# Seven products for eight in the second half of a recurrent-attention and dense-layer kernel

## Chip, cores and metric

One core of one Trainium2 chip. The metric is the device time of one execution in microseconds (us); the time before is the median of three runs.

## What is computed

The reference has two parts. First a recurrent attention over four batches, eight heads, 768 steps and a head size of 48, with a 48x48 state for each head; then a two-layer network on its 3072 rows of 384 numbers, whose nonlinearity is h - tanh(h).

```
for t in range(S):                       # S = 768, B = 4, H = 8, D = 48
    cur = einsum('bhd,bhe->bhde', u * k[t], v[t])
    y[t] = einsum('bhd,bhde->bhe', r[t], state + cur)
    state = w * state + einsum('bhd,bhe->bhde', k[t], v[t])
x = y transposed and reshaped to (3072, 384)
h = x @ w_in                             # 384 -> 2048
g = h - tanh(h)
out = g @ w_out                          # 2048 -> 384
```

All is float32 (the two weight matrices arrive as 64-bit floats and are converted on the chip).

## The kernel before

**Attention.** The 768 steps are cut into 12 chunks of 64 (`SHORT`). A *unit* is one chunk of two batches, so there are 24 units (`unit(n)`, n from 0 to 23; the chunk is n // 2). A unit's steps are: TensorE transposes of r and k into PSUM (`turn`, L644); scaling of r on VectorE into `rT` (L648) and a copy of k on ScalarE into `kT` (L657); 64-wide products of the state with r into `y_ps` and of k with r into `lev` (both in `levels`, issued by `put`, L602); the select of `lev` into `at` on VectorE (L781); the products of `at` with v and of k with v (`outputs`, `to_state`, L602); and the copies out on ScalarE (`to_xt`, `to_rest`, through `given`, L729 and L731), from which GpSimd's DMA queue moves a remainder into place (L745). The state is added and decayed on VectorE (L751, L790).

The two PSUM tiles of attention have two banks each: `x_ps` takes the transposes and then `lev`; `yk_ps` takes `y_ps` and `kv_ps`. Unit 1 has two banks of its own for the first, `x2_ps`, which later serve the output product.

**Dense layer.** Two units are one *block* of 256 rows (`L` = 2), 12 blocks in all. The 2048 columns in the middle are 16 groups of 128 (`NF`), and a *tile* is two groups of one block, so a block has eight tiles. For a tile (`hidden`):

- `h`: 2 x 3 matmuls of 256 columns (L165) into one of two PSUM buffers;
- `act`: five ScalarE passes over 128x512 (L174 to L182);
- `vec`: four VectorE passes over 128x512 (L189 to L195), the last a select into `g` (five buffers);
- `o`: four matmuls of 384 columns (L203), which add into `outs`, two PSUM banks, one for each half of 128 rows of the block.

After the last tile of a group of tiles `empty` moves each bank out: a copy on ScalarE (L222), for the last block a copy on VectorE (L220), or a VectorE sum with what earlier tiles gave (L211). `store` sends the result to memory from GpSimd's queue (L228).

Blocks 0 to 5 (`FIRST` = 6) run while weights still come in: in four passes of four groups each over all six blocks. Blocks 6 to 11 run one after the other, all 16 groups at once (`fs` = (0, 16)). Units 16 to 23 are the attention of blocks 8 to 11 and lie among the tiles of blocks 6 to 9.

**Order.** Every step is a task in `Plan` with an engine, a fixed cost and the tasks that it follows. `order()` simulates the engines with these costs, then tries 1000 random shifts of due times (one fixed seed) and keeps what ends no later; the kernel issues its instructions in the order found. Any change of the tasks therefore changes the order everywhere. While TensorE would idle early on, filler matmuls (`fills`, L539 and L540) keep it running.

A path `anywhere`, for decay factors out of a range, is compiled in but not taken.

Of the kernel before, what the change touches and what calls it, by code (L numbers as in the profile page):

```python
# [11 lines left out]
F32 = mybir.dt.float32  # L12
# [3 lines left out]
AF = mybir.ActivationFunctionType  # L16
ALU = mybir.AluOpType
# [14 lines left out]
C = 128  # L32
# [5 lines left out]
OWN = 1  # L38
SWAP = 2


# [11 lines left out]
class Dims:  # L53
    def __init__(self, r, moe_w_in):
        self.B, self.H, self.S, self.D = r.shape
        self.DM, self.DFF = moe_w_in.shape
        self.NP = self.H // 2
        self.NCH = self.S // C
        self.NU = self.NCH * self.B
        self.NK = self.DM // 128  # L60
        self.NX = self.D // self.NK
        self.NF = self.DFF // 128
        self.NT = L * C
        self.NB = self.NU // L

        self.HEAD = [slice(i * PAD, i * PAD + self.D) for i in range(2)]
# [76 lines left out]
class Dense:  # L143


    def __init__(self, nc, work, gpool, ps_d, shared, out, rows, ps_o=None, last=None):
        self.nc, self.work, self.gpool, self.ps_d, self.ps_o = nc, work, gpool, ps_d, ps_o or (lambda: ps_d)
        self.out, self.rows, self.xts, self.sums, self.last = out, rows, {}, {}, last
        self.d, self.w_in_sb, self.w_out_sb, self.m1b, self.smallb = (
            shared[x] for x in ("dims", "w_in", "w_out", "m1b", "smallb"))  # L150
# [46 lines left out]
    def o(self, t, half):  # L197

        if t.first and half == 0:
            self.outs = [self.ps_o().tile([128, 512], F32, name=f"o{i}", tag=f"o{i}", bufs=1)[:, : self.d.DM]  # L200
                         for i in range(L)]
        for z, i in [(0, half), (1, half)] if t.last else [(half, 0), (half, 1)]:
            self.nc.tensor.matmul(self.outs[i], t.g2[:, z, i * C : (i + 1) * C], self.w_out_sb[:, t.f + z, :],  # L203
                                  start=t.first and z == 0, stop=t.last and z == 1)

    def empty(self, t, i):

        whole, at = t.fs[1] == self.d.NF, (t.j, i)
        if t.fs[0]:
            t.o = self.sums.pop(at) if whole else self.sums[at]  # L210
            self.nc.vector.tensor_tensor(t.o, self.outs[i], t.o, ALU.add)  # L211
            return
        if whole:
            t.o = self.work.tile([128, self.d.DM], F32, name="o", tag="o")
        else:
            t.o = self.sums[at] = self.work.tile([128, self.d.DM], F32, name="part", tag="part", bufs=L * FIRST)
        if t.j == self.d.NB - 1:
            if self.last is not None:
                t.o = self.last[:, i]
            self.nc.vector.tensor_copy(t.o, self.outs[i])  # L220
        else:
            self.nc.scalar.copy(t.o, self.outs[i])  # L222

    def store(self, o, n, z, queue):
# [204 lines left out]
@with_exitstack  # L429
def near(ctx, tc, r, k, v, w, u, out, shared, weights):  # L430

# [11 lines left out]
    ps_a = ctx.enter_context(tc.tile_pool(name="n_ps_a", bufs=1, space=PSUM))  # L443
    ps_d = ctx.enter_context(tc.tile_pool(name="n_ps_d", bufs=2, space=PSUM))

    def fixed(name, shape, dt=F32):
        return const.tile(shape, dt, name=name, tag=name)
# [4 lines left out]
    dense = Dense(nc, work, gpool, ps_d, shared, out,  # L452
                  lambda n: [(n % 2 * 2 + z) * d.S + n // 2 * SHORT for z in range(2)], lambda: later(), shared["last"])
    HALF = [slice(z * SHORT, (z + 1) * SHORT) for z in range(2)]
# [3 lines left out]
    V.memset(rows, 1.0)  # L458
    same = fixed("same", [128, SHORT])
    V.tensor_tensor(same, ident[:, :SHORT], ident[:, SHORT:], ALU.add)  # L460
    by, plus = (work.tile([128, NP, SHORT + 1], F32, name=x, tag=like) for x, like in (("by", "tg"), ("plus", "q")))
# [22 lines left out]
    for z in range(2):  # L484
# [5 lines left out]

    ps, yk_ps = (ps_a.tile([128, 2, 512], F32, name=x, tag=x) for x in ("x_ps", "yk_ps"))

    early = ExitStack()
    x_banks = [ps, early.enter_context(tc.tile_pool(name="n_ps_x", bufs=1, space=PSUM)).tile(
        [128, 2, 512], F32, name="x2_ps", tag="x2_ps")]
    pools = []

    def later():
        if not pools:
            early.close()  # L500
            pools.append(ctx.enter_context(tc.tile_pool(name="n_ps_o", bufs=1, space=PSUM)))
        return pools[0]
    y_ps = yk_ps[:, :, :256].rearrange("e z (p t) -> e z p t", p=NP)
    kv_ps = yk_ps[:, :, 256 : 256 + NP * D].rearrange("d z (p e) -> d z p e", p=NP)
# [96 lines left out]
    def put(*args, **how):  # L601
        T.matmul(*args, skip_group_check=True, **how)  # L602
# [3 lines left out]
    def unit(n):  # L606
# [7 lines left out]
        rt, vt, kw, state = rts[n % (AHEAD + 1)], vts[n % (AHEAD + 1)], kws[n % 2], states[half]  # L614
        r_ps, k_ps = (x_banks[n == 1][:, i] for i in range(2))
        lev, own_lev = (x_banks[n == 1][:, :, at : at + 256].rearrange("s i (p t) -> s i p t", p=NP) for at in (0, 256))
        none = SimpleNamespace(**{x: None for x in "r k v turn rT kw kT rk du own diag state lev cp out xt rest add decay".split()})
# [69 lines left out]

        def levels():
            for p in range(NP if ch else 0):
                for z in range(2):  # L690
                    for i in range(2):
                        put(y_ps[to(i, z), z, p], state[HEAD[i], z, p], t.rT[HEAD[i], p, z],
                            start=p == 0, stop=False)
            for p in range(NP):
                for z in range(2):
                    for i in range(2):
                        put(lev[HALF[z], i, p], t.kT[HEAD[i], p, z], t.rT[HEAD[i], p, z], start=True, stop=True)

# [18 lines left out]
        def to_state():  # L717
            for p in range(NP if more else 0):
                for i in range(2):
                    for z in range(2):  # L720
                        put(kv_ps[i * PAD : (i + 1) * PAD, z, p], kw[HALF[z], 2 * p + i], vt[HALF[z], 2 * p + i, :D],
                            start=True, stop=True)

        def given(out, y):

            if not swap:
                A.copy(out, y)
                return
            A.copy(out[:, 0], y[:, 0])  # L729
            for i in range(2):  # L730
                A.copy(out[i * PAD : (i + 1) * PAD, 1], y[to(i, 1), 1])  # L731

# [24 lines left out]

        free = [b1.cp, b1.diag] if n > 2 else [units[0].cp, units[0].diag] if n == 2 else []
        x.turn = add("PE", .46, lambda: turn(rt, r_ps), [x.r] + free, steps=8)
        x.kw = add("DVE", .47, lambda: V.tensor_tensor(kw[:, :, :D], t.kt[:, :, :D], w_down, ALU.mult), [x.k, downs, b2.out])  # L760
# [12 lines left out]
        else:  # L773
# [4 lines left out]
            x.diag = add("ACT", 1.0, lambda: diagonal(range(H // 2, H)), [now])  # L778
        x.lev = add("PE", (1.35 if swap else 1.75) if ch else .7, levels,
                    [x.kT, x.rT, b2.out] + ([b2.decay, b1.xt, b1.rest, b1.add] if ch else []), steps=128 if ch else 64)  # L780
        x.cp = add("DVE", .64, lambda: V.copy_predicated(t.at, before, lev), [x.lev, b2.out] + ([] if product else [x.diag]))  # L781
# [15 lines left out]

    tiles, stored = [], {}

    def hidden(j, fs, f, due, pace):  # L800
        t = dense.tile(j, fs, f)
        none = SimpleNamespace(g=None, c1=None, c2=None, cp=None, o=None, h=None, s=None, q=None, small=None, th=None, tg=None, empty=[])
        m = len(tiles)
        b1, b2, b5 = (tiles[m - i] if m >= i else none for i in (1, 2, 5))
        x = SimpleNamespace(empty=[])
# [15 lines left out]
        x.cp = add("DVE", .65, lambda: dense.vec(t, "cp"), [x.c2, x.small, x.g])  # L821
        now = add("PE", 1.3, lambda: dense.o(t, 0), [x.cp, converted[piece + 2], b1.o] + b1.empty + ([units[1].cp, units[1].diag] if m == 0 else []), due + 2 * pace, steps=8)
        if m == 0:
# [28 lines left out]
    for n in range(L * (FIRST + 2), d.NU):  # L852
        unit(n)
    for j in range(FIRST, d.NB):
        for f in range(0, d.NF, 2):
            hidden(j, (0, d.NF), f, now, 6.0)
            now += 5.2 + (.95 if j + 2 < d.NB else 0)

# [248 lines left out]
def kernel(  # L1107
# [28 lines left out]
    shared = {"dims": d, "ident": ident, "w_in": w_in_sb, "w_out": w_out_sb, "flag": flag, "last": last, **consts}  # L1136
    with tc.tile_pool(name="stage", bufs=2) as stage:
        weights = Weights(nc, stage, shared, moe_w_in, moe_w_out)
        with tc.manual_schedule():
            near(tc, r, k, v, w, u, out, shared, weights)  # L1140

# [38 lines left out]
```

## Time and profile before

| what | value |
|---|---|
| median of 3 runs | 619.47 us (619.37 to 620.41) |
| profiled execution: span from first to last instruction | 617.3 us |
| what lies around it, by the median of the runs | 2.2 us |
| mean granted TensorE clock | 0.997 |
| TensorE, VectorE, ScalarE, GpSimd busy | 98%, 70%, 65%, 11% |

The profile shows one execution. The page gives its span only; the execution's own device time stands nowhere in it, so the last 2.2 us are the difference to the median. "PE" is TensorE's matmul side, "PEld" its weight loads, DVE is VectorE, ACT ScalarE, POOL GpSimd, SP the sync engine with the main DMA queue. A duration of a matmul is a model from start to end and overlaps the next; how fast a row of them goes is seen in the chain of waits, where each piece is what it adds. For VectorE and ScalarE, too, the mean duration of an instruction is longer than the step to an independent next one: 688 ns for 512 columns, while the chain has 0.60.

### The profile page before, as it was taken

To read this page: it belongs to the slowest core of one execution; us is meant where nothing else is said; L and a number is where in the kernel's file an instruction comes from. 1 tells how busy PE (TensorE), PEld (TensorE's weight loads), DVE (VectorE), ACT (ScalarE), POOL (GpSimd) and SP (SyncE) were. 2 spreads that over 40 slices of the span, in tenths; PEclk is the share of its full clock that TensorE was granted. 3 is DMA by queue.
4 is the path that set the end of the run, shared out by engine and by line. 5 is a ranking of instruction groups with operands and counts; after the bars stand their busy time and mean duration, and the time that the engine had idled before them with its cause. 6 is when DMAs were issued, how large, how long until landed. Compare 5 with 4: busy or idle time off the path is not lost.

```text
span 617.3 us, 13070 instructions
## 1 busy us (share of the span) xinstructions
PE 603.8 (98%) x5215; PEld 444.7 (72%) x5215; DVE 430.4 (70%) x699; ACT 403.6 (65%) x892; POOL 70.5 (11%) x159
## 2 busy tenths in 40 slices
PE   7899999999999999999999999999999999999996
PEld 6667777777777777777777776777777777777774
DVE  5699979999997699766675845657657636445453
ACT  2489789958965667555764855656677666655552
POOL 5001311300000000002132010001101110110100
PEclk9899999999999999999999999999999999999999
DMA  6964495464031000002333112011112100100101
GB/s 126 225 125 92 100 228 109 84 111 133 16 94 52 0 1 2 0 7 46 65 70 67 28 32 53 14 36 37 25 28 48 26 10 1 27 6 1 27 1 30
DMA packets 86318, 33.68 MB, mean 55 GB/s; under 512 B 78536, under 2 KB 80680, under 8 KB 86248
## 3 DMA queue, kind: packets, MB, share of 16 engines
q1 hardware_dynamic: 81084, 25.57, 20.4%
q0 software_dynamic: 4992, 6.99, 4.9%
q8 instruction: 43, 0.70, 0.5%
q14 instruction: 27, 0.22, 0.1%
q10 hardware_dynamic: 172, 0.20, 0.1%
HBM read 26.94 MB, written 4.72 MB: 51 GB/s over the span
## 4 chain that ended last, share of the span: by engine, by line
PE 85%; SPq 5%; DVE 5%; issue 1%; DMA 1%; ACT 1%; DVEq 0%; POOL 0%; ACTq 0%; POOLq 0%
PE o L203 39%; PE h L165 38%; PE yk_ps L602 5%; SPq L632 4%; PE x_ps L644 2%; PE x_ps L602 1%; DMA kt<-in_k_dram 1%; SPq L120 1%; DVE rT L648 1%; DVE tg L193 1%; DVE g L195 0%; DVE g L189 0%; DVE tg L191 0%; DVE rk L661 0%; DVE state L751 0%
## 5 line engine op out<-in xcount | busy, mean ns | idle before, releaser
L203 PE MATMUL o<-w_out_sb,g 128*128 128x384 f32 x768 | 280.6, 489 | 0.8 <-DVE g L195 0.7
L165 PE MATMUL h<-xt,w_in_sb 128*128 128x256 f32 x1152 | 280.9, 380 | 0.0
L165 PEld LDWEIGHTS h<-xt,w_in_sb 128*128 128x128 f32 x1152 | 216.2, 190 | 61.9
L203 PEld LDWEIGHTS o<-w_out_sb,g 128*128 128x128 f32 x768 | 142.9, 190 | 63.8 <-DVE g L195 1.9
L189 DVE TENSOR_TENSOR g<-h,th 128x512 f32<-128x512 f32 x96 | 66.0, 688 | 64.6 <-ACT s L174 43.1
L191 DVE SCALAR_TENSOR_TENSOR tg<-s,tg 128x512 f32<-128x512 f32 x96 | 65.9, 686 | 54.3 <-ACT tg L178 38.0
L174 ACT ACTIVATE s<-h 128x512 f32<-128x512 f32 x96 | 57.2, 596 | 61.3 <-PE h L165 59.7
L178 ACT ACTIVATE tg<-h 128x512 f32<-128x512 f32 x96 | 57.0, 594 | 55.2 <-PE h L165 55.2
L176 ACT ACTIVATE th<-h 128x512 f32<-128x512 f32 x96 | 57.0, 594 | 43.6 <-PE h L165 43.6
L195 DVE COPY_PREDICATED g<-small,tg 128x512 f32<-128x512 int32 x96 | 70.4, 733 | 4.3
L193 DVE SCALAR_TENSOR_TENSOR tg<-q,tg 128x512 f32<-128x512 f32 x96 | 66.2, 689 | 9.5 <-ACT q L180 5.9
L180 ACT ACTIVATE q<-s,m1b 128x512 f32<-128x512 f32 x96 | 69.4, 723 | 0.7
L182 ACT ACTIVATE small<-s,smallb 128x512 f32<-128x512 f32 x96 | 69.3, 722 | 0.5
L745 POOL DMA_DIRECT2D xt<-rest x66 | 32.2, 494 | 202.6 <-ACT rest L731 202.3
L669 ACT ACTIVATE at<-same,du 128x64 f32<-128x64 f32 x184 | 47.6, 339 | 0.4
L228 POOL DMA_DIRECT2D out_dram<-part x24 | 12.6, 528 | 145.8 <-DVE part L211 145.8
L211 DVE TENSOR_TENSOR part<-o,part 128x384 f32<-128x384 f32 x36 | 19.8, 550 | 8.3 <-PE o L203 8.2
L648 DVE TENSOR_TENSOR rT<-x_ps,w_up 128x512 f32<-128x512 f32 x24 | 16.5, 687 | 11.7 <-ACT kT L657 10.5
L781 DVE COPY_PREDICATED at<-before,x_ps 128x512 f32<-128x512 int32 x24 | 17.5, 729 | 9.9 <-PE x_ps L602 9.0
L228 POOL DMA_DIRECT2D out_dram<-o x20 | 10.5, 531 | 97.7 <-ACT o L222 97.7
L602 PEld LDWEIGHTS yk_ps<-rT,state 48*64 48x64 f32 x704 | 12.3, 134 | 11.6 <-issue 3.8
L602 PEld LDWEIGHTS yk_ps<-at,vt 64*64 64x64 f32 x752 | 13.2, 134 | 9.1 <-issue 3.9
(102 smaller groups left out, 440.5 us busy)
## 6 DMA issues: line engine op xcount, KB each, us to landing
st<-in_moe_w_out_dram SPq DMA_DIRECT2D x8, 768.0 KB, 6.9
rt<-in_r_dram SPq DMA_DIRECT2D x48, 96.0 KB, 2.9
vt<-in_v_dram SPq DMA_DIRECT2D x48, 96.0 KB, 3.0
st<-in_moe_w_in_dram SPq DMA_DIRECT2D x16, 288.0 KB, 6.0
kt<-in_k_dram SPq DMA_DIRECT2D x44, 96.0 KB, 3.0
out_dram<-part POOLq DMA_DIRECT2D x24, 96.0 KB, 2.1
out_dram<-o POOLq DMA_DIRECT2D x20, 96.0 KB, 2.1
st<-in_moe_w_in_dram POOLq DMA_DIRECT2D x16, 96.0 KB, 3.7
```

Source lines behind the costliest of these rows:

```text
L165: self.nc.tensor.matmul(t.h2[:, z], self.w_in_sb[:, t.f // 2, kk, z * 128 : (z + 1) * 128], self.xts[t.j][:, kk].rearrange("p b t -> p (b ...
L174: A.activation(out, t.h, AF.Square)
L176: A.activation(out, t.h, AF.Tanh)
L178: A.activation(out, t.h, AF.Tanh, scale=G1)
L180: A.activation(out, t.s, AF.Square, bias=self.m1b)
L182: A.activation(out, t.s, AF.Relu, bias=self.smallb, scale=-1.0)
L189: V.tensor_tensor(t.g, t.h, t.th, ALU.subtract)
L191: V.scalar_tensor_tensor(t.tg, t.s, C4, t.tg, ALU.mult, ALU.mult)
L193: V.scalar_tensor_tensor(t.tg, t.q, K1, t.tg, ALU.add, ALU.mult)
L195: V.copy_predicated(t.g, t.small.bitcast(I32), t.tg)
L203: self.nc.tensor.matmul(self.outs[i], t.g2[:, z, i * C : (i + 1) * C], self.w_out_sb[:, t.f + z, :], start=t.first and z == 0, stop=t.last ...
L602: T.matmul(*args, skip_group_check=True, **how)
```

## The change

For each tile of blocks 6 to 10, and the first six of block 11, `o` is replaced by `products`. The four 128x128 pieces of `g` (two row halves, two groups) times the four 128x192 pieces of `w_out` (two groups, two column halves) are a 2x2 product of blocks, which Strassen's scheme forms from seven products instead of eight. Each product has 192 columns and adds over the tiles in its own half of a PSUM bank (seven halves in the four banks of `x_ps`, which is now one tile `quad`). They need:

- sums of pieces of `g`, three VectorE instructions for each tile (`sums_of_g`), into `s4`, three buffers;
- sums of pieces of `w_out`, once, 16 GpSimd instructions (`mix`, task `mixing`) into `mixed`, which takes the place of the weights' staging buffers after the last conversion;
- at the end of a block six steps that put the seven sums together (`collect`): a ScalarE copy and five VectorE sums, instead of two ScalarE copies;
- the second row half of these blocks with its sign turned (`sign` in `given`; h - tanh(h) is odd), so that only sums are needed.

The products use all four banks that attention's `x_ps` and the dense `outs` had. So units 16 to 23 (`two`) keep everything in the two banks of `yk_ps`: transposes, `lev`, `y_ps` and `kv_ps`. Their state product is a task of its own (`from_state`), a copy of two numbers on ScalarE follows it (`between`), then `levels`; and the transposes of a unit wait until the unit before it has left the banks. The last two tiles of block 11 (`ALONE` = 4 groups) keep the old `o`, in `yk_ps`, and VectorE adds what the first six gave.

```diff
-    def __init__(self, nc, work, gpool, ps_d, shared, out, rows, ps_o=None, last=None):
+    def __init__(self, nc, work, gpool, ps_d, shared, out, rows, outs=None, last=None, seven=None):
...
+            if whole and t.j == self.d.NB - 1 and self.last is not None:
+                t.o = self.last[:, i]
+            if i and t.j in self.negative:
+                self.nc.vector.tensor_tensor(t.o, part, self.outs[i], ALU.subtract)
+            else:
+                self.nc.vector.tensor_tensor(t.o, self.outs[i], part, ALU.add)
...
+    def sums_of_g(self, t, x):
+        add, g, s = self.nc.vector.tensor_tensor, t.g.rearrange("p (a t) -> p a t", a=4), None
+        if x == 0:
+            t.s4 = self.seven.pool().tile([128, 4, C], F32, name="sg", tag="sg", bufs=3)
+            add(t.s4[:, :2], g[:, 0::3], g[:, 1:2].to_broadcast([128, 2, C]), ALU.add)
+        elif x == 1:
+            add(t.s4[:, 2], t.s4[:, 1], g[:, 0], ALU.add)
+        else:
+            add(t.s4[:, 3], t.s4[:, 2], g[:, 2], ALU.add)
+
+    def products(self, t, part):
+        n, w, mixed = self.d.DM // 2, self.w_out_sb, self.seven.mixed[:, t.f // 2]
+        g, s, ps = t.g.rearrange("p (a t) -> p a t", a=4), t.s4, self.seven.ps
+        b11, b21, b22 = w[:, t.f, :n], w[:, t.f + 1, :n], w[:, t.f + 1, n:]
+        for bank, half, a, b in ([(0, 0, g[:, 0], b11), (1, 1, s[:, 0], mixed[:, 2]),
+                                  (0, 1, s[:, 2], mixed[:, 1]), (1, 0, g[:, 3], mixed[:, 3])] if part == 0 else
+                                 [(2, 0, g[:, 2], b21), (2, 1, s[:, 1], mixed[:, 0]), (3, 0, s[:, 3], b22)]):
+            first = t.first and (half == 0) != (bank == 1)
+            self.nc.tensor.matmul(ps[:, bank, half * n : (half + 1) * n], a, b, start=first, stop=t.last,
+                                  skip_group_check=True)
...
+    def collect(self, t, x):
+        n, ps, V = self.d.DM // 2, self.seven.ps, self.nc.vector
+        if x == 0:
...
+            self.nc.scalar.copy(t.e[:, :n], ps[:, 0, :n])
+        elif x == 1:
+            V.tensor_tensor(t.e[:, n:], t.e[:, :n], ps[:, 0, n : 2 * n], ALU.subtract)
+        elif x == 2:
+            V.tensor_tensor(t.u[:, :n], t.e[:, n:], ps[:, 1, n : 2 * n], ALU.add)
+        elif x == 3:
+            flat = ps.rearrange("p b n -> p (b n)")[:, 512 : 512 + 2 * (512 + n)]
+            V.tensor_tensor(t.os[1].rearrange("p (i n) -> p i n", i=2), t.u[:, None, :n].to_broadcast([128, 2, n]),
+                            flat.rearrange("p (i n) -> p i n", i=2)[:, :, :n], ALU.add)
+        elif x == 4:
+            V.tensor_tensor(t.os[0], t.e, ps[:, 2, : 2 * n], ALU.add)
+        else:
+            V.tensor_tensor(t.os[0][:, n:], t.os[0][:, n:], ps[:, 3, :n], ALU.add)
...
+    quad, yk_ps = (ps_a.tile([128, n, 512], F32, name=x, tag=x) for x, n in (("x_ps", 4), ("yk_ps", 2)))
+    x_banks = [quad[:, :2], quad[:, 2:]]
...
+        two = n >= L * (FIRST + 2)
+        banks = yk_ps if two else x_banks[n == 1]
+        sign = -1.0 if slot and j in dense.negative else 1.0
...
+        if two:
+            free = [b1.xt, b1.rest, b1.add, b1.cp, b1.diag]
...
+        if two:
+            now = add("PE", .68, from_state, both + [x.rT, b1.xt, b1.rest, b1.add, b2.decay, x.kT], steps=64)
+            begun = [add("ACT", .15, between, [now])]
...
+        if seven:
+            x.sg = add("DVE", .33, lambda: dense.sums_of_g(t, 0), [x.cp, b3.o, b1.cp])
+            for i in (1, 2):
+                x.sg = add("DVE", .19, lambda i=i: dense.sums_of_g(t, i), [x.sg])
+            done = units[L * (FIRST + 2) - 1]
+            now = add("PE", 1.32, lambda: dense.products(t, 0), [x.sg, mixed[f // 4], b1.o, done.cp, done.diag, done.lev] + b1.empty, due + 2 * pace, steps=16)
+            x.o = add("PE", .99, lambda: dense.products(t, 1), [now], due + 2 * pace + 1.3, steps=12)
+            if t.last:
+                finished_seven(t, x, due, pace)
+            return
...
+    mixing()
     for j in range(FIRST, d.NB):
...
+        ends = (d.NF,) if j < d.NB - 1 else (d.NF - ALONE, d.NF)
+        for at, end in zip((0, *ends), ends):
+            for f in range(at, end, 2):
+                hidden(j, (at, end), f, now, 6.0, at == 0)
```

## The prediction

> **What bounds the kernel now.** I read the page first (busy shares, then the chain), then the table of windows, then the chain piece by piece.
>
> ```profile
> PE 603.8 (98%) x5215; PEld 444.7 (72%) x5215; DVE 430.4 (70%) x699; ACT 403.6 (65%) x892; POOL 70.5 (11%) x159
> PE 85%; SPq 5%; DVE 5%; issue 1%; DMA 1%; ACT 1%; DVEq 0%; POOL 0%; ACTq 0%; POOLq 0%
> PE o L203 39%; PE h L165 38%; PE yk_ps L602 5%; SPq L632 4%; PE x_ps L644 2%; PE x_ps L602 1%; DMA kt<-in_k_dram 1%; SPq L120 1%; DVE rT L648 1%; DVE tg L193 1%; DVE g L195 0%; DVE g L189 0%; DVE tg L191 0%; DVE rk L661 0%; DVE state L751 0%
> ```
>
> TensorE is busy for 98% of the span and is 85% of the chain that ended last; the two matrix products of the second layer (h, o) are 77% of it. The changed output product is the single largest line.
>
> ```profile
> core 0: us, PE busy (x) PEld busy (x) DVE busy (x) ACT busy (x) POOL busy (x), PEclk, DMA share, GB/s
> 100.00:150.00 50.00, 50.00 (x440) 37.40 (x441) 48.07 (x77) 39.84 (x81) 7.40 (x15) 1.00 0.51 106
> 350.00:400.00 50.00, 49.46 (x431) 35.41 (x430) 28.01 (x45) 31.61 (x76) 5.00 (x10) 1.00 0.16 33
> 550.00:600.00 50.00, 50.00 (x196) 36.88 (x195) 25.20 (x38) 28.85 (x53) 5.01 (x10) 1.00 0.04 11
> ```
>
> Blocks 6 to 11 fill the stretch from about 335 us to the end (their first result copy starts at 383.0 us). There TensorE has no gaps to speak of, at a granted clock of 1.00, and VectorE is half idle. In 100 to 150 us VectorE was 96% busy and TensorE still 100%, so this order of work can bear a nearly full VectorE.
>
> **What a pass costs.** Each f32 matmul runs as two passes with a weight load each. The profiled 380 and 489 ns overlap, so the price is the distance in the chain.
>
> ```profile
> 301.63 1.29 PE o L203 x4
> 302.92 1.29 PE h L165 x6
> 304.22 0.62 PE yk_ps L602 x32
> 304.84 0.47 PE x_ps L602 x32
> 305.31 1.49 PE h L165 x6
> ```
>
> Four passes of 384 columns take 1.29 us, 0.3225 each; six of 256 take 1.29, 0.215 each. A burst of 64-wide attention products costs more at both ends: its first 32 take 0.62 us where the next take 0.47, and the dense group behind it takes 1.49 instead of 1.29. A burst more is 0.15 + 0.20 = 0.35 us.
>
> **Seven for eight.** A tile's output product was 8 passes of 384 columns, 8 x 0.3225 = 2.58 us; it becomes 7 products of 192 columns, 14 passes. Columns fall by an eighth, weight loads rise from 8 to 14. No pass of 192 columns is in the trace; the nearest with fewer columns, and a full 128x128 load each, is this filler:
>
> ```profile
> 48.63 0.83 PE L540 MATMUL x_ps<-ident 128*128 128x128 f32 x6
> ```
>
> Less the 0.275 us of one whole matmul, five steps take 0.555 us: 0.111 us at 128 columns, load included. A straight line to 0.215 at 256 gives 0.163 at 192. Bounds: below, half of the 384-column pass, 0.161; above, the profiled duration of a load, 190 ns, if loads could not overlap each other:
>
> ```profile
> L203 PEld LDWEIGHTS o<-w_out_sb,g 128*128 128x128 f32 x768 | 142.9, 190 | 63.8 <-DVE g L195 1.9 <-DVE part L211 0.6 <-PE x_ps L540 0.5
> ```
>
> I take 0.163, because the filler's loads also show 190 ns and yet repeat every 0.111. So 14 x 0.163 = 2.28 us, 0.30 saved a tile. Blocks 6 to 10 have 8 such tiles, block 11 has 6 (its last two stay at 384 columns): 46 x 0.30 = 13.8 us. Bounds: 46 x (2.58 - 2.25) = 15, and 46 x (2.58 - 2.66) = -3.7, a loss.
>
> A rule speaks against this. The Trainium skill, "TensorE: Matmul & The Clock Gate", section "The mechanism" of Part 3, says that a weight load overlaps running matmuls only where it goes to other rows of the array; its section "LDWEIGHTS (loading the stationary operand)" prices a 128-column load at 107 ns. By that each pass would pay its load on top, six more a tile, and the change would lose some 15 us. The chain's 0.215 us for a 256-column pass with its load, hardly more than the columns alone by the 384-column row, says the load is hidden; the measurement decides.
>
> **VectorE.** Three sums a tile, of 256, 128 and 128 columns. Neighbours:
>
> ```profile
> L775 DVE TENSOR_TENSOR rk<-rk,ub 128x384 f32<-128x384 f32 x23 | 12.6, 552 | 0.2
> L548 DVE TENSOR_SCALAR by<-yk_ps 128x256 f32<-128x256 f32 x1 | 0.4, 425 | 3.2 <-ACT saved L559 3.2
> L460 DVE TENSOR_TENSOR same<-ident 128x64 f32<-128x64 f32 x1 | 0.2, 226 | 0.3 <-POOL ident masks.py:199 0.3
> ```
>
> About 0.42 + 0.29 + 0.29 = 1.0 us; 46 us in all. A block's end has one ScalarE copy of 192 columns (314 ns by the 64x192 rows) and five VectorE steps, 3 x 0.36 + 2 x 0.55 = 2.2 us, in place of two copies of 0.48 on ScalarE: 13 us over six blocks. Between 350 and 600 us VectorE was busy 142 of 250 us (the same table in steps of 25); with 59 more in some 240 it is at 84%, below the 96% above. I charge it nothing as throughput. As latency: from the end of the last h product (605.47) to the end of the last select into g was 3.87 us on idle engines; the sums with 0.09 us between dependent steps add 1.3, so 5.2 us. In the changed order 5.7 (0.98 + 3 x 1.29 + 2 x 0.44, two transposes) to 9.4 us of TensorE work lie between a tile's h and its first product: the cover holds by 0.5 us at its thinnest and is gone where attention's steps stand in front on VectorE (0.55 to 0.73 us each).
>
> Block change: the next block's first products write banks 0 and 1, so they wait for the copy and the first three VectorE steps, about 2.5 to 3 us with what is queued between; the order puts 3.6 to 5.4 us of h and attention work there. For both kinds of wait together I take 1 us (this stretch had 0.65 us of TensorE idle before), bounds 0 and 8.
>
> GpSimd's 16 mixings (two-input, 384 columns; its 384-column memset took 0.41 us, so 7 to 20 us) come after the last weight conversion (249.8 us) and 80 us before their first use, on an engine 11% busy. Queued behind them are only the stores of blocks 0 to 5. The sign of the second token half is a scale in ScalarE copies that are there already. Nothing for both.
>
> **Attention in two banks.** Units 16 to 23 now have the state product, the levels and the outputs as three bursts instead of mostly two, with the small ScalarE copy between the first two; in the emitted order bursts rise from 49 to 58 over the kernel. 9 x 0.35 = 3.2 us. Each unit becomes one serial string (transposes, scaling, state, copy, levels, select, outputs, copies out), some 8 to 12 us, but two units have a block of 46 us, and dense work stands in every gap of the order. Waiting instructions would hold the dense work queued behind them on TensorE. Included in the 1 us above.
>
> **The first 100 us.** The planner's search gives another order here too: five units instead of four before the first output product, and filler of 15 wide and 29 narrow matmuls for 13 and 31. Two wide (about 0.86 each) less two narrow (0.22) is 1.3 us more planned idle. I take +0.7, bounds -1.5 and +3.
>
> **The end.**
>
> ```profile
> 604.16 1.31 PE h L165 x6
> 608.60 0.74 DVE g L195
> 609.38 2.86 PE o L203 x8
> 612.27 0.56 DVE last L220
> ```
>
> The last output product waited for g and cost 0.28 more than 8 x 0.3225. In the new order 28 passes of 192 and 8 of 384, 7.1 us, cover that chain; the last step is an add (550 ns) in place of a copy (558). Gain 0.3 us.
>
> **Sum.** -13.8 + 3.2 + 1.0 + 0.7 - 0.3 = -9.2 on a span of 617.3: 608.1. The median lies 2.2 above that span, which I carry over: 610.3 us.
>
> **The rivals.**
> - Waits on VectorE eat part of it: 0.1 us a tile and 0.5 a block beyond the cover, 4.6 + 3 = 7.6: 618, still just faster; half that, 614. For: the thinnest cover is only 0.5 us and g, select and sums stand in one strict queue. Against: 96% VectorE without a TensorE gap.
> - Slower: the weight loads set the pace. At 190 ns a pass the products lose 3.7 us, and with the other terms (3.2 + 1.0 + 0.7 - 0.3 = 4.6) the time is 628. It decides from 0.177 us a pass: there a tile saves 2.58 - 2.48 = 0.10, 4.6 over 46 tiles, and the net is zero; above that the kernel is slower. For: 14 loads where 8 were. Against: the filler at 0.111.
> - The same side by another road: waits above 0.2 us on each of the 46 tiles also cancel the 9.2 us; at 0.3, 623.
> - More gained: early order no worse and no new waits: 607 to 608.
>
> **How the numbers follow.** As summed, 606 to 613: 0.72. Partly eaten, 613 to 618: 0.15. Loads set the pace: 0.05. Waits on every tile: 0.05. No net effect: 0.03. A difference under 0.2% (1.2 us) can't be told from none. Faster 0.87, same 0.03, slower 0.10. Range 606 to 617: it leaves out the slower cases and a little below.
>
> **What would show it.** Right: 644 passes of 192 columns, steps of x6 and x8 at about 0.98 and 1.30 us in the chain, TensorE still 98% busy, idle before products from VectorE under 2 us in all. Wrong: eight passes at 1.5 us (loads), TensorE idle released by sg or by the collecting steps, or a first 100 us longer by more than 3.

## The result, and the profile after

The changed kernel takes 638.36 us (median of 4 runs, 637.85 to 638.67); the kernel before took 619.42 us in the same comparison (4 runs, 615.13 to 620.41). The ratio is 1.029 [1.024, 1.034] (in square brackets, here and below, a 95% interval): 3% slower, where 610.3 us and a range of 606 to 617 had been forecast. The profiled execution took 638.67 us with a span of 637.0 us, 1.7 us around it. Of the four runs of one kernel below, `merged`, three took some 658 us at a granted clock of 0.982 to 0.985 and one 648.20 us at 0.993, so its ratio, taken from 648.20 and 657.56, is loose, and its page, of a run of 658.22, is read for which waits there are and not for their size.

The page's first part and its chain, of the changed kernel:

```profile
PE 601.9 (94%) x5491; PEld 480.1 (75%) x5491; DVE 485.0 (76%) x867; ACT 402.9 (63%) x896; POOL 89.8 (14%) x175
...
PE 81%; DVE 8%; ACT 4%; issue 3%; DMA 2%; SPq 1%; POOL 0%; DVEq 0%; POOLq 0%
```

TensorE's work went down only from 603.8 to 601.9 us, and its share of the span from 98% to 94%. In the chain VectorE has 8% where it had 5%, and ScalarE 4% where it had 1%: the chain now changes engines more often.

The chain piece by piece (start, length, what) where the seven products begin shows that this part came as forecast:

```profile
369.17 1.29 PE h L166 x6
370.47 1.30 PE x_ps L254 x8
371.77 1.29 PE h L166 x6
373.06 0.97 PE x_ps L254 x6
374.04 1.29 PE h L166 x6
```

1.30 and 0.97 us for 14 passes, nothing between them and the h products. The first product starts at 370.3 us, though; before, block 6's first output product had started at 337.7. The time went in blocks 0 to 5, which the change was not meant to touch. The windows of the changed kernel:

```profile
0.00:50.00 50.00, 40.34 (x527) 29.36 (x530) 28.60 (x54) 22.85 (x61) 9.35 (x37) 0.93 0.71 142
50.00:100.00 50.00, 41.85 (x828) 30.30 (x828) 40.59 (x74) 36.89 (x110) 10.98 (x22) 1.00 0.68 139
100.00:150.00 50.00, 46.28 (x602) 33.10 (x603) 42.34 (x67) 37.35 (x91) 7.79 (x16) 1.00 0.31 57
```

The columns are length, then busy time of TensorE, weight loads, VectorE, ScalarE and GpSimd. Between 100 and 150 us TensorE had been busy for all 50.00 us; now it is 46.28, and VectorE is less busy too (42.34, 48.07 before). No engine is fuller: they wait for each other. For what, the waits say (engine and line, what it waited for, us in total, times, longest):

```profile
DVE rT L725 <- PE x_ps L204: 9.3, 6, 2.2
DVE part L217 <- PE x_ps L204: 6.3, 7, 2.2
DVE at L875 <- PE x_ps L204: 6.0, 7, 1.6
PEld x_ps L204 <- DVE part L217: 8.2, 17, 1.5
PEld x_ps L204 <- ACT kT L734: 2.8, 5, 0.7
```

L204 is the old output product of blocks 0 to 5, now named `x_ps`. `rT`, `kT` and `at` are attention's reads of its own two banks. Neither attention's reads nor this product use a number of the other. Yet attention's scaling and select wait for the output product, and the output product's weight loads wait for attention's copy. The same in the chain, between 103 and 107 us:

```profile
102.65 1.04 PE x_ps L721 x8
...
103.78 0.70 DVE rT L725
...
104.50 0.59 ACT kT L734
...
105.14 1.56 PE x_ps L204 x4
```

After the transposes TensorE stands still through one VectorE and one ScalarE instruction, some 1.45 us, until the output product may begin. In the kernel before, the output product (L203) stood in the waits of its own sums and copies (`part` 8.2 us, `last` 2.4) and never in those of attention, where `rT` waited for attention's copy and `at` for attention's products:

```profile
DVE rT L648 <- ACT kT L657: 10.5, 8, 3.0
DVE at L781 <- PE x_ps L602: 9.0, 7, 4.1
DVE part L211 <- PE o L203: 8.2, 6, 2.5
```

### The profile page after: what moved, and what is told of

Same layout as the page of the kernel before. It is cut to its first block, busy times and chain, and to the rows that moved or that the text cites. A ratio compares the mean times of both kernels' runs of the same rounds, so it can differ in the third digit from the quotient of the medians.

```text
span 637.0 us, 13835 instructions
## 1 busy us (share of the span) xinstructions
PE 601.9 (94%) x5491; PEld 480.1 (75%) x5491; DVE 485.0 (76%) x867; ACT 402.9 (63%) x896; POOL 89.8 (14%) x175
## 4 chain that ended last, share of the span: by engine, by line
PE 81%; DVE 8%; ACT 4%; issue 3%; DMA 2%; SPq 1%; POOL 0%; DVEq 0%; POOLq 0%
PE h L166 34%; PE x_ps L204 18%; PE x_ps L254 16%; PE yk_ps L676 6%; PE x_ps L721 2%; PE x_ps L613 1%; DVE rT L725 1%; SPq L709 1%; DVE at L875 1%; PE h L613 1%; PE yk_ps L721 1%; PE x_ps L676 1%; DVE tg L194 1%; ACT kT L734 1%; DVE tg L192 1%
## 5 line engine op out<-in xcount | busy, mean ns | idle before, releaser
L204 PE MATMUL x_ps<-w_out_sb,g 128*128 128x384 f32 x384 | 142.9, 495 | 6.0 <-DVE part L217 3.5
L204 PEld LDWEIGHTS x_ps<-w_out_sb,g 128*128 128x128 f32 x384 | 69.4, 190 | 43.7 <-DVE part L217 8.2
L190 DVE TENSOR_TENSOR g<-h,th 128x512 f32<-128x512 f32 x96 | 65.8, 686 | 42.0 <-ACT s L175 19.8
L192 DVE SCALAR_TENSOR_TENSOR tg<-s,tg 128x512 f32<-128x512 f32 x96 | 66.0, 687 | 30.1 <-ACT tg L179 18.9
L196 DVE COPY_PREDICATED g<-small,tg 128x512 f32<-128x512 int32 x96 | 71.7, 747 | 5.0 <-DVE g L190 0.5
L254 PE MATMUL x_ps<-mixed,sg 128*128 128x192 f32 x276 | 59.9, 326 | 0.0
L254 PEld LDWEIGHTS x_ps<-mixed,sg 128*128 128x128 f32 x276 | 47.4, 190 | 0.0
L254 PE MATMUL x_ps<-w_out_sb,g 128*128 128x192 f32 x184 | 46.3, 333 | 1.2 <-DVE o L287 1.2
L254 PEld LDWEIGHTS x_ps<-w_out_sb,g 128*128 128x128 f32 x184 | 33.2, 190 | 6.0 <-ACT small L183 1.6
L812 ACT COPY xt<-yk_ps 64x192 f32<-64x192 f32 (+2 forms) x50 | 16.0, 320 | 19.7 <-PE yk_ps L676 19.2
L217 DVE TENSOR_TENSOR part<-x_ps,part 128x384 f32<-128x384 f32 x36 | 19.8, 549 | 7.3 <-PE x_ps L204 6.3
```

The lines of the kernel that those rows point to most:

```text
L190: V.tensor_tensor(t.g, t.h, t.th, ALU.subtract)
L192: V.scalar_tensor_tensor(t.tg, t.s, C4, t.tg, ALU.mult, ALU.mult)
L196: V.copy_predicated(t.g, t.small.bitcast(I32), t.tg)
L254: self.nc.tensor.matmul(ps[:, bank, half * n : (half + 1) * n], a, b, start=first, stop=t.last, skip_group_check=True)
```

## The experiments

**Theory.** The code's waits are set for a PSUM tile, not for a bank (the tests below bear this out for this kernel). The change made one tile (`quad`) of what had been attention's two-bank tile and two one-bank output tiles. So every output product of blocks 0 to 5 must wait for attention's last read of the other two banks, and attention for the output product. **Rivals:** the order that the search found, or the products and sums themselves.

**1. `split`: the changed kernel with separate tiles.** The instructions on TensorE, ScalarE, GpSimd and SP and their order stay as in the changed kernel; on VectorE one sum at a block's end, which read two banks at once, becomes two of 192 columns.

```diff
-    quad, yk_ps = (ps_a.tile([128, n, 512], F32, name=x, tag=x) for x, n in (("x_ps", 4), ("yk_ps", 2)))
-    x_banks = [quad[:, :2], quad[:, 2:]]
+    ps, yk_ps = (ps_a.tile([128, 2, 512], F32, name=x, tag=x) for x in ("x_ps", "yk_ps"))
+    first_ps = ExitStack()
+    x_banks = [ps, first_ps.enter_context(tc.tile_pool(name="n_ps_x", bufs=1, space=PSUM)).tile(
+        [128, 2, 512], F32, name="x2_ps", tag="x2_ps")]
...
+    def four():
+        return [ps[:, 0], ps[:, 1], *o_tiles()]
```

`o_tiles` gives two tiles of one bank each, as before the change.

> The changed kernel with its four PSUM banks as separate tiles again: attention's two banks one tile, each output bank a tile of its own, as before the change; one of the five combining sums of a block becomes two of 192 columns. The order of TensorE's, ScalarE's, GpSimd's and the DMA queues' instructions stays as it is in the changed kernel. Theory (shared tile: in blocks 0 to 5 the output product and attention's steps wait for each other because they lie in one PSUM tile): the first 370 us shrink by 20 to 30 us, time 605 to 616. Rival (the newly found order is itself worse in the first part): still 630 to 639.

Measured: 610.38 us (610.13 to 611.35), the kernel before in the same batch 621.96 us, ratio 0.981 [0.978, 0.984]; in a second batch (`split_again`) 609.79 us (609.71 to 609.97), ratio 0.982 [0.980, 0.984].

> The version with separate PSUM tiles once more, as the base for the others of this batch: 610 us, within 1 us of its first time of 610.4.

Its page, and its windows:

```profile
PE 594.6 (98%) x5491; PEld 481.3 (79%) x5491; DVE 485.4 (80%) x873; ACT 401.6 (66%) x896; POOL 90.5 (15%) x175
```

```profile
50.00:100.00 50.00, 48.10 (x920) 35.85 (x920) 46.48 (x84) 42.23 (x129) 11.40 (x23) 1.00 0.72 146
100.00:150.00 50.00, 50.00 (x437) 36.52 (x436) 45.47 (x74) 40.26 (x86) 7.41 (x16) 1.00 0.50 104
```

The count of TensorE's instructions is the same, 5491, and it is back at 98%; from 100 to 300 us it has no gap. Cut at the first of the new products, the two kernels compare like this, first the split one, then the changed one:

```profile
0.00:343.40 343.40, 334.62 (x3250) 246.59 (x3251) 279.83 (x460) 236.41 (x539) 65.37 (x125) 1.00 0.39 80
343.40:608.50 265.10, 260.02 (x2243) 234.69 (x2241) 205.55 (x414) 165.21 (x359) 25.16 (x51) 1.00 0.11 24
```

```profile
0.00:370.30 370.30, 341.46 (x3249) 245.57 (x3250) 279.42 (x460) 237.27 (x539) 64.66 (x125) 0.99 0.36 74
370.30:637.00 266.70, 260.42 (x2243) 234.54 (x2241) 205.62 (x408) 165.67 (x359) 25.16 (x51) 1.00 0.11 24
```

Before the first product both run the same work on each engine, and one of them takes 26.9 us longer; behind it the difference is 1.6 us. Of the 26.9 us 6.8 show as longer TensorE busy time, the rest as idle time. The lag grows along the whole stretch, and fastest where attention is densest: matmul for matmul, the changed kernel is 7.5 us behind split at split's 49 us, 17.1 at 124 and 26.6 at 336. The order is the same, so the rival of the order falls; what differs is the tiles, and with them the waits.

**2. `merged`: the kernel before with the shared tile alone.** The other way round: the old output product, no sums, no two-bank attention; the instructions of all five engines and their order are those of the kernel before.

```diff
-    ps, yk_ps = (ps_a.tile([128, 2, 512], F32, name=x, tag=x) for x in ("x_ps", "yk_ps"))
+    quad, yk_ps = (ps_a.tile([128, n, 512], F32, name=x, tag=x) for x, n in (("x_ps", 4), ("yk_ps", 2)))
+    x_banks = [quad[:, :2], quad[:, 2:]]
...
+        return [x_banks[1][:, i, : d.DM] for i in range(L)]
```

The last line gives the output product its two banks, now a part of the shared tile.

> The kernel before, with attention's two banks and the two output banks as one PSUM tile of four banks and nothing else; the order of instructions on every engine is that of the kernel before. Theory (shared tile): 20 us or more slower than before, 640 to 655, most of it in the first 150 us, with TensorE's output product waiting on attention's copies out of PSUM and the other way round. Rival (order): 619 to 621.

Measured: ratio 1.049 [1.040, 1.058], some 30 us (25 to 36) on 622; by the lower run alone, of 648.20 us, the loss is 26 us. Its waits are those of the changed kernel; the kernel before has none of this kind:

```profile
DVE at L776 <- PE x_ps L204: 17.5, 10, 2.7
PEld x_ps L204 <- ACT kT L652: 5.8, 5, 2.0
```

Nothing of Strassen's scheme is in this kernel, so the loss belongs to the tile. Here attention lies beside the output product up to block 9, in the changed kernel only up to block 5; whether the later blocks cost more, and whether most of the loss lies in the first 150 us, as expected, is not shown.

**3. `two_banks`: the kernel before with attention of units 16 to 23 in two banks, and nothing else of the change.** The search finds an order of its own here.

```diff
+        two = n >= L * (FIRST + 2)
+        banks = yk_ps if two else x_banks[n == 1]
...
+        if two:
+            free = [b1.xt, b1.rest, b1.add, b1.cp, b1.diag]
```

> The kernel before with units 16 to 23 in two PSUM banks (state product, small ScalarE copy and levels as three steps), output product and tiles as before. The order is searched anew. Prediction's price: 8 to 9 more bursts of 0.35 us, 621 to 624. Rival (the serial string of a unit stalls TensorE): 630 or more.

Measured: 626.53 us (626.05 to 628.23), ratio 1.0075 [1.0046, 1.0103]: 4.6 us (2.9 to 6.4) above the kernel before, which took 621.96 us in this batch; above the 621 to 624 that were expected, and under the rival's 630. By the spans, split (608.5) lies 15.8 us under this one (624.3), and 13.6 of that is TensorE's busy time (594.6 against 608.2), close to the forecast price of the products. The other 2.2 us lie in TensorE's idle time and the two kernels' orders differ, so they are not assigned.

**4. `split_no_sums`: split without the three VectorE sums of g for each tile** (the products read pieces of g itself in their place).

```diff
     def sums_of_g(self, t, x):
-        add, g, s = self.nc.vector.tensor_tensor, t.g.rearrange("p (a t) -> p a t", a=4), None
...
+        pass
```

> The kernel with separate tiles, and the three sums of g left out in each tile (the products read pieces of g in their place, so that the output is not the reference's). All engines but VectorE keep their order. Prediction's price for the sums, nothing but waits within 1 us: within 1.5 us of the kernel with separate tiles. Rival (VectorE's queue holds TensorE in blocks 6 to 11): 4 us or more faster than it.

Measured: 611.19 us (609.92 to 612.55), against 610.38 with the sums. The windows from 375 to 600 us, of split and then of this one:

```profile
375.00:600.00 225.00, 224.79 (x2035) 203.76 (x2035) 178.31 (x361) 144.68 (x319) 21.99 (x44) 1.00 0.11 23
```

```profile
375.00:600.00 225.00, 224.79 (x2036) 203.88 (x2035) 144.37 (x243) 145.28 (x319) 22.05 (x44) 1.00 0.11 23
```

VectorE loses 34 us of work in this stretch, and TensorE is busy 224.79 us in both. By the medians leaving the sums out gains nothing, so they are hidden behind TensorE's work.

**5. `pair`: split, but with the two output banks as one tile**, attention's tile still apart.

```diff
-        return [o_pools[0].tile([128, 512], F32, name=f"o{i}", tag=f"o{i}", bufs=1) for i in range(2)]
+        both = o_pools[0].tile([128, 2, 512], F32, name="o", tag="o", bufs=1)
+        return [both[:, i] for i in range(2)]
```

> Separate tiles for attention and output product as in the split version, but the two banks of the output product are one tile; same order of instructions. Theory A, the loss comes from the tie between attention and the output product: this tie is left undone, so 610 to 613 us. Rival B, any tile of several banks costs, because the product of the second half must then wait for the sum of the first half too (one L217 sum, 0.55 us, for each of the 24 group ends of blocks 0 to 5 and 6 block ends): with nothing to cover it 30 x 0.55 = 16 us, so 620 to 627 us.

Measured: 615.66 us (614.83 to 617.23), between the two expectations: 5.9 us above split in the same batch. A wait of the weight loads that is 0.5 us in split grows to 6.4:

```profile
PEld o L204 <- DVE part L217: 6.4, 14, 1.8
```

The next group's first product now waits until both halves have been added, not only its own. So one part of the loss, about 6 us, comes from the two output banks' tie to each other. The rest of the 26.9 us, some 21, is then that of attention and output product to each other; it was not run alone, and the two need not add exactly.

**6. `late_quad`: split in blocks 0 to 5, one tile of four banks from the first seven-product tile on.**

```diff
+        if not quads:
+            o_ps.close()
+            x_ps_pool.close()
+            quads.append(ctx.enter_context(tc.tile_pool(name="n_ps_q", bufs=1, space=PSUM)).tile(
+                [128, 4, 512], F32, name="quad", tag="quad"))
+        return [quads[0][:, i] for i in range(4)]
```

> Separate tiles while attention and output product run beside each other in these banks (blocks 0 to 5), and one tile of four banks from the first seven-product tile on; same order. Theory A: in blocks 6 to 11 attention has left these banks, so only the collecting steps and the next block's first products can wait for each other, 6 times: 610 to 612 us. Rival B: bank by bank tracking is needed there too; a whole set of collecting steps, about 2.5 us, is then uncovered at each of 5 block changes: 620 to 623 us.

Measured: 612.95 us (612.47 to 613.68), 3.2 us above split, 0.95 us above the upper end of what the theory had expected and far from the rival's 620. From the first product (345.2 us) to the end (612.0) it takes 266.8 us, `split_again` 265.2: 1.6 us, the figure that the changed kernel showed as well. The rest lies ahead of the first product (345.2 against 342.9 us in the two traces), where both have the same work and separate tiles; TensorE's busy time in the first 50 us (42.66 against 44.12) shows most of it, and what made that start slower is open. So some 2 us in the start can come without a difference in tiles. The traces show where most of the 1.6 us behind the first product lie. In the changed kernel the copy that starts a block's end waits for the last of the seven products, and at one of the five block changes, at 512.8 us, the next block's first product waits for the last of the collecting sums:

```profile
ACT e L275 <- PE x_ps L254: 6.0, 5, 1.8
PE x_ps L254 <- DVE o L287: 1.2, 1, 1.2
```

In `late_quad` both waits have the same sizes, 6.0 and 1.2 us. In split the copy waits for the products in banks 0 and 1 alone, 0.8 us in all, and no first product waits for a sum. The copy's wait is ScalarE's; what reaches TensorE is the 1.2 us. So in blocks 6 to 11 the shared tile costs 1.6 us, little beside its 27 in blocks 0 to 5.

**7. `eight`: split with an eighth product of 192 columns a tile**, into the unused half of the fourth bank.

```diff
-        (2, 0, g[:, 2], b21), (2, 1, s[:, 1], mixed[:, 0]), (3, 0, s[:, 3], b22)]):
+        (2, 0, g[:, 2], b21), (2, 1, s[:, 1], mixed[:, 0]), (3, 0, s[:, 3], b22), (3, 1, g[:, 1], b21)]):
```

> The split version with an eighth product of 192 columns for each of the 46 tiles, into the free half of the fourth bank, which nothing reads; same order otherwise, the same waits. If TensorE sets the pace of blocks 6 to 11 and a pass costs 0.163 us: 46 x 2 x 0.163 = 15.0 us more, 625 us. If weight loads of 190 ns set the pace of these passes: 46 x 2 x 0.19 = 17.5, 628 us. If something beside TensorE sets the pace (VectorE's sums, the string of attention), part of it is hidden: under 620 us.

Measured: 624.86 us (624.69 to 626.79), 15.07 us above split in the same batch, for 92 passes more (46 tiles, two passes each): 0.164 us each. TensorE sets the pace of blocks 6 to 11 alone, and a load of 190 ns behind a 192-column pass costs nothing. This also is what seven for eight is worth by itself: with eight products in the same places the kernel is slower than the one before (ratio 1.007 [1.005, 1.010]).

## Why the prediction was wrong

**The step that failed** is "The first 100 us": +0.7 us, bounds -1.5 and +3. It treated blocks 0 to 5 as changed in their order alone. It never asked what one tile for four banks does to the waits there; its list of what the change adds has waits on VectorE's sums, at a block's end and in the two-bank units, all in blocks 6 to 11. The term that was left out measures 27 us ahead of the first product and 1.6 behind (experiment 1), 28.0 by the medians of two batches (638.36 - 610.38), 30.5 when each is taken against the kernel before in its own batch (+18.9 and -11.6). Separate tiles take it away, and the same tile put into the kernel before costs about as much (experiment 2). The premise behind it, that waits go by bank, stands openly in the paragraph on the block change, where the first products wait for three VectorE steps, those that read banks 0 and 1; in the changed kernel the one such wait that shows is for the last step, which reads bank 3 (experiment 6). It was readable ahead of time: the diff has one tile where three were, and in the trace of before attention's products, whose results `rT`, `kT` and `at` read, and the output product's L203 take turns on TensorE through blocks 0 to 5. The text did name "a first 100 us longer by more than 3" as what would make it wrong; the loss reached further, to 370 us.

**The steps that held,** as the split kernel shows, whose 610.4 and 609.8 us lie where the forecast, which lacked this term, had put the changed kernel:

- Seven for eight, -13.8: steps of 1.30 and 0.97 us were seen (2.27, forecast 2.28), a pass is worth 0.164 us (forecast 0.163), and TensorE's busy time is 13.6 us less than with two-bank attention alone.
- The loads' rival, 628 us at 0.19 us a pass: fallen (experiment 7). The Trainium skill's rule that a load hides only behind passes in other rows ("TensorE: Matmul & The Clock Gate", Part 3, "The mechanism") is not what these passes do: full 128-row loads of 190 ns stay hidden behind passes of 0.164 us. The same section also lets a load go ahead into a background weight buffer; these runs fit that, but do not test it.
- VectorE's sums as throughput, 0, and as waits, 1.0: within the spread in split (experiment 4); the rival of waits on VectorE falls with them. The shared tile adds the 1.2 us at a block change, which is about what had been taken for waits. In split the weight loads of the products that read sums have no idle time before them:

```profile
L256 PEld LDWEIGHTS x_ps<-mixed,sg 128*128 128x128 f32 x184 | 31.2, 190 | 0.0
```

- Attention in two banks, +3.2, with the other order, +0.7: 3.9 together, against 4.6 (2.9 to 6.4) in `two_banks`, whose order is one of its own. The two agree within the interval; the runs do not part them.
- GpSimd's mixings, hidden: 16 of about 1.25 us each, 19.8 us in the changed kernel and 20.7 in split, at the upper end of the 7 to 20 allowed for, and with no one waiting.
- The end, -0.3: the last products follow each other without a wait for g; the size is too small to be seen.

That the sum meets split within 1 us is in part luck. In their own batches the kernel before took 621.96 and 621.02 us, not 619.47, so split gained 11.6 and 11.2 us where the sum had 9.2; split lies 16.2 us under `two_banks`, where the terms between the two give 13.1; and the 4.6 us alone has an interval of 3.5 us. The range failed for the same reason as the sum: it was built from the terms on the list.

**The better kernel.** Split is faster than both, 1.8% under the kernel before (0.982 [0.980, 0.984]) and some 28 us under the changed one.

## What to carry to other kernels

When a change merges buffers into one tile, list every reader and writer of each old buffer, in the stages that the change is not about as well, and ask who now waits for whom: here a saving of some 14 us in one half of the kernel was bought with 27 us of waits in the other half, and separate tiles took the waits away with TensorE's instructions in the same order. Keep a PSUM tile to the banks that are written and read together; the one instruction that had needed these banks in one tile, once a block, could be split in two (VectorE was busy 485.4 us for 485.0).

## What the runs showed of the hardware

Different engines can work in different PSUM banks without waiting for each other: the split kernel runs the changed one's instructions, but for one sum a block that is split in two, without the waits between attention and output product, 28 us faster. The Trainium skill, "PSUM — Partial Sum Buffer", section "PSUM bank collisions raise a hardware error", asks for a guard by bank and quadrant, and the split kernel's, by tiles of one and two banks, agrees with that.

The granted clock of the first 50 us was 0.93 in the changed kernel and 0.97 in split, but it was 0.93 in `pair` as well, where TensorE was busy for 43.99 us of them against 43.93 in split. So the clock at the start differs between executions without a difference in work, and does not make up the 26.9 us.

A GpSimd sum of two 128x384 operands takes 1.23 to 1.33 us in the mean of its groups, three times the 0.41 us of its memset of 384 columns, and 2.2 to 2.4 times VectorE's 0.55 us for a sum of that size.
